# Ten more probability tiles split by GpSimd, weight subtractions cut in halves, and the first pair's bit rows copied by ScalarE, in a fused attention and MoE kernel

## The chip, the cores and the metric

The kernel runs on one core of one Trainium2 chip, as one program. The metric is the device time of one execution in microseconds. The kernel before took 852.72 us (median of 3 executions, 852.25 to 853.36).

## What is computed

Three layers follow each other. The first is attention in which a query sees only the keys that fall into the same hash bucket; the second and third are two feed-forward layers. Inputs are float32; 2 batches, 8 heads, 768 positions, head size 64.

```python
q_bits = (np.einsum('bhsd,dk->bhsk', q, proj) > 0)      # 6 bits, k_bits alike
mask = q_bucket[:, :, :, None] == k_bucket[:, :, None, :]
scores = np.where(mask, scale * np.matmul(q, k.transpose(0, 1, 3, 2)), -1e9)
attn = np.exp(scores - scores.max(-1, keepdims=True))
attn = attn / (attn.sum(-1, keepdims=True) + 1e-09)
x = np.matmul(attn, v)
...
xn = x / np.sqrt(np.mean(x * x, -1, keepdims=True) + 1e-06) * rms_g
x = (silu(xn @ w_gate) * (xn @ w_val)) @ w_out          # 512 -> 1536 -> 512
...
out = elu(x @ w_in) @ w_out                             # 512 -> 2048 -> 512
```

## The kernel before

**Split numbers.** TensorE multiplies operands of type float32r. Where full accuracy is wanted, a float32 tile is split into a rounded upper part (made by a cast) and the rest (made by a subtraction), and products are summed over two or three passes. So nearly every tile that goes to TensorE needs a cast, mostly on ScalarE, and a subtraction, mostly on VectorE.

**Attention.** Two heads make a pair, eight pairs in all (`j`). `prep` makes the operands of a pair: `twice` copies a head's rows next to themselves into `rd` (L334); `prep_T` transposes halves of `rd` on TensorE (L350), ScalarE makes the upper part `tq` or `tk` from the PSUM bank (L356), VectorE the rest (L361), and GpSimd copies the lower half of `tq` into two further places, `again` (L368) and `across` (L371). `prep_bits` and `prep_count` compute the hash bits and turn them into extra rows of the operands (L398 to L430), so that scores in other buckets come out far too small. The bits of a pair need all `across` copies of that pair.

A pair has six units `u`, each of two score tiles of 128 x 768. For each tile TensorE computes scores (L477), VectorE the row maximum `nm` (L484), ScalarE the exponential `p` (L494). Then `turn` transposes the unit's probabilities in three pieces `n` (L522), and each piece is split into `pt`: ScalarE casts it from PSUM (L530) and VectorE subtracts (L534). The pieces `n == 0` of the units listed in `BYPOOL` go another way: ScalarE copies the bank to SBUF as `pf` (L539), GpSimd casts (L543) and subtracts (L546). `weigh` multiplies with the values (L569), three pieces into one PSUM bank, in the order 1, 2, 0 for the units in `BYPOOL`; ScalarE and VectorE join the halves into `ot` (L583, L587). `post` scales by the reciprocal sums `r` (L605, L610) and `norm` makes the normed activations `xn` of a batch: for the first batch on GpSimd (L699 to L746), while the pairs 4 and 5 run, for the second on VectorE and ScalarE after pair 7.

**Feed-forward.** Eleven groups of hidden columns. `weights` loads a float64-wide tile, brings it to float32 with one instruction of ScalarE (L811) and four of VectorE (L814, L820, L827, L834, all within SBUF), then splits it: ScalarE casts (L855), GpSimd subtracts (L859). The weights of the first group are converted while the last three pairs run. `hidden` (L908 to L958), `reduce1` (L993) and `reduce2` (L1048) follow.

**Order.** Every piece of work is given to `Plan.add` with its engine, an estimated duration, what it reads and writes, and a priority. `Plan.order` is a list scheduler that runs in Python when the program is built: it keeps a clock for each engine, starts whatever can start first, breaks ties by priority, and the instructions are issued in that order, which is fixed for each engine's in-order queue. The table `OFF` shifts priorities by kind of work and pair. PSUM has four single banks (`bank`) and two double ones; `pt` has four buffers, the half-size pool `h3` nine.

Of the kernel before, what the change touches and what calls it, by code (L numbers as in the profile page):

```python
# [24 lines left out]
POOL_COPY = 0.82  # L25
FIRST = ('Pool', 'DVE', 'Pool', 'ACT')
# [3 lines left out]
BYPOOL = ([0, 1, 2, 3, 4], [0, 2, 3, 4], [0, 1, 2, 3, 4, 5], [2, 4], [2, 4], [2, 4], [2, 4], [0])  # L30
HOT = ('DVE', 'ACT', 'ACT', 'DVE')
BW = (384, 512)
OFF = {'S': [-0.746, -0.843, -1.864, 66.85, -0.744, -0.758, -0.224, -0.41], 'max': [86.06, 128.957, 190.513, 53.124, 102.143, -5.035, -10.834, 24.749], 'exp': [119.567, 67.059, 76.291, 2.774, 75.069, 56.662, -35.846, 43.868], 'T': [0.573, 0.48, 0.307, 0.831, 0.703, 1.127, 1.259, 1.321], 'hi': [36.303, -33.663, 1.961, -57.136, 22.322, 57.959, -91.469, -121.974], 'lo': [-34.121, 9.653, 32.465, -109.77, -12.636, -87.223, -67.192, -11.818], 'V': [2.027, 1.953, 1.894, 2.015, 1.865, 2.222, 2.417, -11.303], 'my': [76.979, -114.216, -55.16, -8.134, -134.423, -45.978, -63.486, -29.752], 'ld': [16.116, 103.645, 134.666, -130.684, 51.199, 277.906, -45.786, 44.455], 'pv': [19.903, -68.605, 49.828, -156.296, 63.827, 116.499, -168.838, 19.653], 'prep': [-0.809, -2.78, -3.346, -0.341, -0.21, -0.194, 0.226, -82.459], 'post': [4.851, 4.774, 2.643, 1.592, 3.332, 9.244, 3.712, 28.29], 'plo': [-227.264, -10.728, 0.013, -54.307, -64.379, -36.39, 74.399, -48.961], 'wc': 0.693, 'ld1': 50.459, 'norm0': -125.474, 'rush': 27.318, 'pstep': 0.316, 'qstep': 0.146, 'norm': -8.853, 'w0': 189.461, 'w0s': 3.7229545865993564e+29}


class Plan:

# [142 lines left out]
def kernel(  # L180
# [1086 lines left out]
```

## Time and profile before

| | us |
|---|---|
| median of 3 executions | 852.72 |
| the profiled execution's own time | 852.93 |
| its span, first to last instruction | 851.1 |
| TensorE busy | 832.4 (98%) |
| VectorE busy | 638.5 (75%) |
| ScalarE busy | 444.9 (52%) |
| GpSimd busy | 273.3 (32%) |

The 1.8 us between span and time lie before the first and after the last instruction. The shares are means over two very different stages: attention, to about 290 us, in which three or four engines are busy nearly all the time, and the feed-forward layers, in which TensorE runs almost alone. They have to be read stage by stage.

### The profile page before, as it was taken

Reading aid. Unit: us, or ns where it says so; the run is one execution under the profiler, and the core shown is the slowest. Engines: PE = TensorE matmul, PEld = TensorE weight load, DVE = VectorE, ACT = ScalarE, POOL = GpSimd, SP = SyncE. Lnnn points to the kernel's source line nnn. Section 1 sums busy time; section 2 is a strip of 40 time slices with the busy share of each in tenths; the row PEclk is TensorE's granted clock in tenths of the full one; section 3 lists DMA queues with packets and bytes.
Section 4 is the critical chain, followed back from the end, with each engine's and each line's share of the span. In section 5 each row is a group of like instructions: output and inputs, shape, how many; then the busy total and the mean of one; then the engine's idle time right before and its main releaser. Section 6 shows DMA issues by size and latency. Waiting matters only on the chain.

```text
span 851.1 us, 12464 instructions
## 1 busy us (share of the span) xinstructions
PE 832.4 (98%) x4722; PEld 736.7 (87%) x4722; DVE 638.5 (75%) x1015; ACT 444.9 (52%) x838; POOL 273.3 (32%) x289
## 2 busy tenths in 40 slices
PE   8999999998999999999999999999999999999998
PEld 7999999887998899999889898887888888888786
DVE  6999899999999987534364565579857778676754
ACT  6988988898987664432222322235444333332321
POOL 7857476789824312111011111110201101111100
PEclk9999999999999999999999999999999999999999
DMA  5102012330002200310111312213121302001003
GB/s 168 41 17 75 2 38 75 121 122 1 20 1 75 75 13 26 112 50 1 56 48 46 100 50 100 75 33 128 62 75 37 112 25 75 25 30 46 1 12 137
DMA packets 25708, 49.05 MB, mean 58 GB/s; under 512 B 2480, under 2 KB 8880, under 8 KB 25648
## 3 DMA queue, kind: packets, MB, share of 16 engines
q1 hardware_dynamic: 25648, 48.25, 17.3%
q8 instruction: 37, 0.61, 0.3%
q14 instruction: 23, 0.19, 0.1%
HBM read 45.09 MB, written 3.15 MB: 57 GB/s over the span
## 4 chain that ended last, share of the span: by engine, by line
PE 81%; DVE 13%; ACT 4%; issue 1%; POOL 1%; ACTq 0%; DVEq 0%; POOLq 0%
PE ps_h L908 37%; PE ps_o L1048 14%; PE ps_y L993 11%; PE ps_p L522 5%; PE ps_v L569 5%; PE ps_s L477 4%; DVE nm L484 3%; DVE pt L534 3%; PE ps_t L350 2%; PE ps_b L398 2%; ACT p L494 1%; ACT pt L530 1%; DVE wf L827 1%; DVE wf L834 1%; PE ps_w L1153 1%
## 5 line engine op out<-in xcount | busy, mean ns | idle before, releaser
L859 POOL TENSOR_TENSOR wlo<-wf,whi 128x768 fp32r<-128x768 f32 (+1 forms) x54 | 86.8, 1607 | 442.9 <-ACT whi L855 430.6
L908 PE MATMUL ps_h<-xn,whi 128*128 128x512 f32 (+2 forms) x768 | 190.2, 337 | 0.8 <-DVE hf L939 0.7
L908 PEld LDWEIGHTS ps_h<-xn,whi 128*128 128x128 f32 x768 | 133.5, 189 | 13.2 <-DVE hf L939 1.1
L908 PE MATMUL ps_h<-xn,wlo 128*128 128x256 f32 (+2 forms) x384 | 128.9, 336 | 0.0
L1048 PE MATMUL ps_o<-whi,h 128*128 128x512 f32 (+1 forms) x388 | 118.7, 387 | 0.8 <-DVE oa L1060 0.8
L908 PE MATMUL ps_h<-y,whi 128*128 128x512 f32 x384 | 118.2, 389 | 0.0
L933 ACT ACTIVATE sg<-ps_h 128x512 f32<-128x512 f32 (+1 forms) x87 | 50.7, 583 | 116.6 <-PE ps_h L908 114.5
L855 ACT CAST whi<-wf 128x768 fp32r<-128x768 f32 (+1 forms) x54 | 39.6, 733 | 118.2 <-DVE wf L834 118.2
L569 PE MATMUL ps_v<-pt,vv 128*128 128x256 f32 x576 | 96.8, 295 | 4.1 <-DVE pt L534 3.2
L954 ACT CAST h<-hf 128x512 fp32r<-128x512 f32 (+1 forms) x87 | 51.6, 605 | 88.1 <-DVE hf L939 49.1
L993 PE MATMUL ps_y<-h,whi 128*128 128x512 f32 (+1 forms) x312 | 91.4, 374 | 1.5 <-DVE ya L1005 1.5
L484 DVE TENSOR_REDUCE nm<-ps_s 128x1 f32<-128x768 f32 x96 | 90.6, 945 | 1.6 <-PE ps_s L477 0.9
L958 DVE TENSOR_TENSOR h<-hf,h 128x512 fp32r<-128x512 f32 (+1 forms) x87 | 71.0, 831 | 26.9 <-ACT h L954 26.2
L494 ACT ACTIVATE p<-ps_s,nm 128x768 f32<-128x768 f32 x96 | 87.2, 909 | 5.5 <-DVE nm L484 4.4
L522 PE MATMUL ps_p<-ident,p 128*128 128x128 f32 x576 | 86.0, 275 | 3.3 <-DVE pt L534 1.5
L477 PE MATMUL ps_s<-tk,tq 128*128 128x384 f32 x384 | 87.9, 350 | 0.6 <-ACT tk L428 0.4
L1048 PEld LDWEIGHTS ps_o<-whi,h 128*128 128x128 f32 x388 | 72.2, 188 | 16.4 <-DVE oa L1060 1.9
L569 PEld LDWEIGHTS ps_v<-pt,vv 128*128 128x128 f32 x576 | 79.3, 189 | 7.2 <-DVE pt L534 5.1
L908 PEld LDWEIGHTS ps_h<-y,whi 128*128 128x128 f32 x384 | 72.1, 188 | 15.0
L939 DVE TENSOR_TENSOR hf<-ps_h,sg 128x512 f32<-128x512 f32 (+1 forms) x39 | 25.2, 647 | 78.5 <-PE ps_h L908 78.5
L534 DVE TENSOR_TENSOR pt<-ps_p,pt 128x512 fp32r<-128x512 f32 x120 | 79.9, 680 | 2.7 <-ACT pt L530 1.8
L908 PEld LDWEIGHTS ps_h<-xn,wlo 128*128 128x128 f32 x384 | 72.6, 189 | 5.5
(111 smaller groups left out, 1501.0 us busy)
## 6 DMA issues: line engine op xcount, KB each, us to landing
wraw<-in_moe_w_out_dram SPq DMA_DIRECT2D x12, 768.0 KB, 4.9
wraw<-in_moe_w_in_dram SPq DMA_DIRECT2D x8, 768.0 KB, 4.6
wraw<-in_moe_w_out_dram SPq DMA_DIRECT2D x10, 512.0 KB, 4.1
raw<-in_q_dram SPq DMA_DIRECT2D x16, 192.0 KB, 3.4
raw<-in_k_dram SPq DMA_DIRECT2D x16, 192.0 KB, 3.7
vn<-in_v_dram SPq DMA_DIRECT2D x8, 384.0 KB, 3.3
wraw<-in_moe_w_gate_dram SPq DMA_DIRECT2D x4, 768.0 KB, 4.4
wraw<-in_moe_w_val_dram SPq DMA_DIRECT2D x4, 768.0 KB, 4.6
```

The costliest lines, as they stand in the source:

```text
L477: nc.tensor.matmul(st[B_][:, hf, 0:HS], lhsT=tq[:, x, c * 128:(c + 1) * 128], rhs=tk[:, x, hf * HS:(hf + 1) * HS], start=(x == 0), stop=(x ...
L484: nc.vector.tensor_reduce(out=st["nm", u, cc], in_=st[B_][:, :, 0:HS], axis=AX.XY, op=ALU.max, negate=True,)
L494: nc.scalar.activation(out=halves(st["p", u][:, cc]), in_=st.pop(B_)[:, :, 0:HS], func=AF.Exp, bias=st["nm", u, cc], scale=1.0, accum_out= ...
L522: nc.tensor.transpose(out=st[B_][:, o:o + 128], in_=p[:, cc, (2 * n + kt) * 128:(2 * n + kt + 1) * 128], identity=ident,)
L534: nc.vector.tensor_tensor(out=pt[:, 1], in0=st.pop(B_), in1=f(pt[:, 0]), op=ALU.subtract)
L569: nc.tensor.matmul(st[B_][:, 0:256], lhsT=st["vv", j][:, a, 2 * n + kt, :], rhs=pt[:, x, kt * 256:(kt + 1) * 256], start=(n == seq[0] and ...
L859: nc.gpsimd.tensor_tensor(out=l, in0=s["w"], in1=f(h), op=ALU.subtract)
L908: nc.tensor.matmul(ps[:, o:o + ln], lhsT=w[wp][:, kk, ft * 128:(ft + 1) * 128], rhs=t[xp][:, s:s + ln], start=(kk == 0 and n == 0), stop=( ...
L954: nc.scalar.copy(out=st["h", g, blk, ft][:, 0, 0:bw], in_=s["hf"])
L958: nc.vector.tensor_tensor(out=h[:, 1, 0:bw], in0=s["hf"], in1=f(h[:, 0, 0:bw]), op=ALU.subtract)
L993: nc.tensor.matmul(s["ps"][:, 0:bw], lhsT=wo[wp][:, ft, m * 128:(m + 1) * 128], rhs=h[:, xp, 0:bw], start=(ft == 0 and i == 0), stop=(ft = ...
L1048: nc.tensor.matmul(s["ps"], lhsT=h[:, xp, t * 128:(t + 1) * 128], rhs=wo[wp][:, ft, ds], start=(ft == 0 and i == 0), stop=(ft == n - 1 and ...
```

## The change

Five things are changed. (1) `BYPOOL` lists ten more units: pairs 3 to 7 have 3, 3, 4, 6 and 3 instead of 2, 2, 2, 2 and 1. (2) The subtraction of the weights on GpSimd (L859) is issued as two instructions over half a tile each. (3) In pair 0 the `across` copies are made by ScalarE from the PSUM bank, not by GpSimd from SBUF, and VectorE's subtraction for `tk` then covers 64 partitions. (4) In pair 0 the four `twice` copies are made by VectorE, ScalarE, ScalarE, VectorE instead of GpSimd, VectorE, GpSimd, ScalarE. (5) VectorE tasks whose operands all lie in SBUF are entered in the plan with 0.2 us more (`port=True`); with other entries of `OFF` and some other estimates this gives another order on every engine. `AGAIN` and `NORM` keep what was done before.

```diff
-POOL_COPY = 0.82
-FIRST = ('Pool', 'DVE', 'Pool', 'ACT')
+POOL_COPY = 0.79
+FIRST = ('DVE', 'ACT', 'ACT', 'DVE')
...
-BYPOOL = ([0, 1, 2, 3, 4], [0, 2, 3, 4], [0, 1, 2, 3, 4, 5], [2, 4], [2, 4], [2, 4], [2, 4], [0])
+BYPOOL = ([0, 1, 2, 3, 4], [0, 2, 3, 4], [0, 1, 2, 3, 4, 5], [1, 2, 4], [1, 3, 5], [0, 2, 4, 5], [0, 1, 2, 3, 4, 5], [0, 1, 4])
+AGAIN = ('Pool', 'Pool', 'Pool', 'Pool', 'Pool', 'Pool', 'Pool', 'Pool')
+ACROSS = ('ACT', 'Pool', 'Pool', 'Pool', 'Pool', 'Pool', 'Pool', 'Pool')
+NORM = ('Pool', 'DVE')
...
-OFF = {'S': [-0.746, -0.843, -1.864, 66.85, ...
+OFF = {'S': [-1.867, -1.487, -1.644, 46.711, ...
...
+    SHARED = 0.2
...
+        if port and eng == "DVE":
+            self.tasks[i] = (eng, us + self.SHARED, *self.tasks[i][2:])
...
-            m = (up, slice(0, 128))[i]
+            m = up if i == 0 else dn if ACROSS[j] == "ACT" else slice(0, 128)
...
-        def across():
-            nc.gpsimd.tensor_copy(out=operand(j, a, 1)[up, 1, cs], in_=f(operand(j, a, 0)[dn, 0, cs]))
+        def under():
+            to = operand(j, a, 1)[up, 1, cs]
+            if ACROSS[j] == "ACT":
+                nc.scalar.activation(out=to, in_=st[B_][up, 0:HS], func=AF.Copy, scale=sc)
+            else:
+                nc.gpsimd.tensor_copy(out=to, in_=f(operand(j, a, 0)[dn, 0, cs]))
...
-        def lo():
+        def lo(x):
             h, l = (wpart(t, g, m, part) for t in st["w", g][nm])
-            nc.gpsimd.tensor_tensor(out=l, in0=s["w"], in1=f(h), op=ALU.subtract)
+            if shape[1] % 2 == 0:
+                z = (slice(None), slice(x * shape[1] // 2, (x + 1) * shape[1] // 2))
+            else:
+                z = (slice(None), slice(None), slice(x * shape[2] // 2, (x + 1) * shape[2] // 2))
+            nc.gpsimd.tensor_tensor(out=l[z], in0=s["w"][z], in1=f(h[z]), op=ALU.subtract)
```

Two places show how the order moves. The first is GpSimd's queue behind the norm of batch 0, in pairs 4 and 5: `xn` ends the norm, `pt` is a probability tile (cast, then subtraction), `tq` and `tk` are the copies that the bits of pair 6 wait for. Before:

```order
L746 TENSOR_TENSOR xn<-xT,xn 128x384
L543 CAST pt<-pf 128x512
L746 TENSOR_TENSOR xn<-xT,xn 128x384
L546 TENSOR_TENSOR pt<-pf,pt 128x512
L543 CAST pt<-pf 128x512
L368 CAST tq<-tq 64x384
L546 TENSOR_TENSOR pt<-pf,pt 128x512
L368 CAST tq<-tq 64x384
L371 CAST tk<-tq 64x384 x2
L368 CAST tq<-tq 64x384 x2
L371 CAST tk<-tq 64x384 x2
```

With the change:

```order
L767 TENSOR_TENSOR xn<-xT,xn 128x384 x2
L564 CAST pt<-pf 128x512 x2
L567 TENSOR_TENSOR pt<-pf,pt 128x512 x2
L564 CAST pt<-pf 128x512
L377 CAST tq<-tq 64x384
L567 TENSOR_TENSOR pt<-pf,pt 128x512
L564 CAST pt<-pf 128x512
L639 COPY rw<-r 128x768
L567 TENSOR_TENSOR pt<-pf,pt 128x512
L377 CAST tq<-tq 64x384
L384 CAST tk<-tq 64x384 x2
L377 CAST tq<-tq 64x384 x2
```

Four tiles instead of two, and the copy `rw`, now stand between the norm and the `tk` copies (two more of which follow the last row shown).

The second is VectorE's queue from behind the last row maximum of attention to the last probability tiles: `wf` are the conversions of the weights, `hf` belongs to the first hidden unit. Before:

```order
L827 SCALAR_TENSOR_TENSOR wf<-wraw,wf 128x768
L820 TENSOR_SCALAR wf<-wf 128x768
L605 TENSOR_SCALAR r<-sums 128x12
L834 SCALAR_TENSOR_TENSOR wf<-wraw,wf 128x768
L610 RECIPROCAL r<-r 128x12
L827 SCALAR_TENSOR_TENSOR wf<-wraw,wf 128x768
L587 TENSOR_TENSOR ot<-ps_v,ot 64x256
L939 TENSOR_TENSOR hf<-ps_h,sg 128x384
L814 TENSOR_SCALAR wf<-wf 128x768
L834 SCALAR_TENSOR_TENSOR wf<-wraw,wf 128x768
L534 TENSOR_TENSOR pt<-ps_p,pt 128x512 x3
```

With the change:

```order
L835 TENSOR_SCALAR wf<-wf 128x768
L555 TENSOR_TENSOR pt<-ps_p,pt 128x512
L608 TENSOR_TENSOR ot<-ps_v,ot 64x256
L555 TENSOR_TENSOR pt<-ps_p,pt 128x512
L841 TENSOR_SCALAR wf<-wf 128x768
L626 TENSOR_SCALAR r<-sums 128x12
L848 SCALAR_TENSOR_TENSOR wf<-wraw,wf 128x768
L631 RECIPROCAL r<-r 128x12
L855 SCALAR_TENSOR_TENSOR wf<-wraw,wf 128x768
L608 TENSOR_TENSOR ot<-ps_v,ot 64x256
L967 TENSOR_TENSOR hf<-ps_h,sg 128x384
L555 TENSOR_TENSOR pt<-ps_p,pt 128x512 x3
```

Four conversions instead of six stand there, and none between `hf` and the last three tiles.

## Rows read from the trace of the kernel before

**Rows 1.** Busy time by 25 us: PE, PEld, DVE, ACT, POOL (instructions), clock, DMA.

```profile
175.00:200.00 25.00, 21.60 (x153) 18.84 (x151) 24.54 (x40) 24.72 (x53) 22.74 (x23) 1.00 0.22 71
200.00:225.00 25.00, 23.38 (x164) 21.22 (x164) 23.87 (x40) 21.61 (x45) 23.56 (x29) 1.00 0.05 16
225.00:250.00 25.00, 24.55 (x181) 23.32 (x181) 24.76 (x41) 21.79 (x47) 10.57 (x15) 1.00 0.00 1
250.00:275.00 25.00, 23.04 (x170) 21.95 (x169) 24.76 (x37) 19.40 (x40) 11.54 (x7) 1.00 0.20 65
275.00:300.00 25.00, 23.00 (x146) 21.71 (x146) 24.75 (x37) 16.20 (x27) 8.87 (x5) 1.00 0.19 64
```

**Rows 2.** Groups of TensorE, 225 to 300 us: busy, mean ns | idle before, releaser.

```profile
L569 PE MATMUL ps_v<-pt,vv 128*128 128x256 f32 x144 | 24.1, 296 | 3.2 <-DVE pt L534 3.2
L522 PE MATMUL ps_p<-ident,p 128*128 128x128 f32 x136 | 19.6, 274 | 0.3 <-DVE xT L636 0.3
L908 PE MATMUL ps_h<-xn,whi 128*128 128x384 f32 x64 | 16.7, 341 | 0.8 <-DVE hf L939 0.7
L477 PE MATMUL ps_s<-tk,tq 128*128 128x384 f32 x73 | 16.5, 345 | 0.1
L908 PE MATMUL ps_h<-xn,wlo 128*128 128x384 f32 x32 | 10.7, 335 | 0.0
```

**Rows 3.** Chain that ended last, 244 to 305 us: start, duration, what.

```profile
271.81 2.11 PE ps_h L908 x12
273.93 1.43 PE ps_v L569 x12
275.35 0.70 PE ps_s L477 x4
276.06 1.32 PE ps_p L522 x12
...
285.01 2.52 DVE wf L834
```

**Rows 4.** Groups of VectorE, 214.9 to 284 us, first row maximum of pair 6 to `hf`.

```profile
L534 DVE TENSOR_TENSOR pt<-ps_p,pt 128x512 fp32r<-128x512 f32 x35 | 23.1, 679 | 0.2
...
L827 DVE SCALAR_TENSOR_TENSOR wf<-wraw,wf 128x768 int32<-128x768 int32 x4 | 3.7, 929 | 0.0
```

**Rows 5.** Groups of GpSimd, 0 to 300 us.

```profile
L546 POOL TENSOR_TENSOR pt<-pf,pt 128x512 fp32r<-128x512 f32 x24 | 32.3, 1348 | 1.3
...
L543 POOL CAST pt<-pf 128x512 fp32r<-128x512 f32 x24 | 15.4, 642 | 41.2 <-ACT pf L539 38.1 <-ACT pt L530 2.1 <-POOL tk L371 0.6
```

**Rows 6.** Timeline of GpSimd, 163 to 208 and 284 to 289 us: start, duration, instruction.

```profile
163.78 1.01 POOL L699 TENSOR_TENSOR z<-z,y 128x384 f32<-128x384 f32 x1 [1.17 <-ACT y L694]
...
197.23 1.02 POOL L746 TENSOR_TENSOR xn<-xT,xn 128x384 fp32r<-128x384 f32 x1
198.20 2.17 POOL L546 TENSOR_TENSOR pt<-pf,pt 128x512 fp32r<-128x512 f32 x1
...
205.81 1.59 POOL L371 CAST tk<-tq 64x384 fp32r<-64x384 f32 x2
...
284.79 1.92 POOL L859 TENSOR_TENSOR wlo<-wf,whi 128x768 fp32r<-128x768 f32 x1 [0.62 <-ACT whi L855]
```

**Rows 7.** One line of VectorE, L605, whole span: duration ns min/median/max.

```profile
L605 DVE TENSOR_SCALAR r<-sums x8: 161/242/1209, 47.1 to 281.5; 128x12 f32<-128x12 f32 x8
```

**Rows 8.** Timeline of ScalarE and TensorE in the first 13 us.

```profile
4.63 0.84 ACT L1115 ACTIVATE bitt<-ident 1x768 fp32r<-1x768 f32 x1
5.80 0.83 ACT L334 COPY rd<-raw 128x768 f32<-128x768 f32 x1 [0.32 <-DMA raw<-in_k_dram]
...
9.71 0.87 ACT L356 ACTIVATE tq<-ps_t 128x384 fp32r<-128x384 f32 x2
...
12.61 0.44 PE L398 MATMUL ps_b<-tk,pj 128*128 128x384 f32 x1 [0.56 <-POOL tk L371]
```

More of the change, by code (lines that the diff above doesn't have):

```diff
@@ L50, in __init__, with add @@
         self.last_w, self.readers, self.touch, self.duty = {}, {}, {}, {}
-    def add(self, eng, us, fn, r=(), w=(), prio=None, lat=0.0, tab=None, duty=1.0):
+    def add(self, eng, us, fn, r=(), w=(), prio=None, lat=0.0, tab=None, duty=1.0, port=False):
         i = len(self.tasks)
@@ L336, in twice @@
         us = {"Pool": POOL_COPY, "DVE": dve(S), "ACT": act(S) + 0.04}[eng]
-        plan.add(eng, us, go, [(("slot", "raw", j), i, a)], [("h3", "rd", j, a, i)], prio)
+        plan.add(eng, us, go, [(("slot", "raw", j), i, a)], [("h3", "rd", j, a, i)], prio, port=eng == "DVE")
     def prep_T(j, a, i, hf, prio):
@@ L612, in post @@
         sums = [(("sum", j), a, c) for a in range(2) for c in range(NC)]
-        plan.add("DVE", 0.1, plus, sums, [R_], prio)
-        plan.add("DVE", 0.17, inv, [], [R_], prio)
+        plan.add("DVE", 0.08, plus, sums, [R_], prio, port=True)
+        plan.add("DVE", 0.14, inv, [], [R_], prio, port=True)
         def widen():
@@ L751, in norm @@
                 if late:
-                    plan.add("DVE", dve(HS) + 0.06, scale, [(Y_, hf), "gsc"], [F_], p + step)
+                    plan.add("DVE", dve(HS) + 0.06, scale, [(Y_, hf), "gsc"], [F_], p + step, port=True)
                 else:
@@ L914, in wkeys @@
     def wkeys(g, m):
-        return [(("slot", x, g, m), p) for x in ("whi", "wlo") for p in range(2)]
+        return [(("slot", "whi", g, m), p) for p in range(2)] + [
+            (("slot", "wlo", g, m), p, x) for p in range(2) for x in range(2)
+        ]
     def hidden(g, blk, ft, prio):
@@ L1025, in reduce1 @@
             plan.add("ACT", act(bw) + 0.043, hi, ak, [*yk[0], (Y_[1], "got", blk)], prio)
-            plan.add("DVE", dve(bw), lo, ak + yk[0], yk[1], prio)
+            plan.add("DVE", dve(bw), lo, ak + yk[0], yk[1], prio, port=True)
     def reduce2(g, blk, t, prio):
@@ L1140 @@
     plan.add("Pool", 1.22, setup, [], ["ident", "pj0"], -30)
-    plan.add("DVE", 0.7, setup_w, [], [("h3", "wtmp")], -30)
-    plan.add("DVE", 2.2, setup_count, [("h3", "wtmp")], [("h3", "ctmp")], -30)
+    plan.add("DVE", 0.5, setup_w, [], [("h3", "wtmp")], -30, port=True)
+    plan.add("DVE", 1.0, setup_count, [("h3", "wtmp")], [("h3", "ctmp")], -30, port=True)
     plan.add("Pool", 0.25, setup2, [], ["wsel0"], -29.5)
@@ L1156 @@
         plan.add("PE", 0.218, lambda n=n: warm(n), ["ident"], [("bank", "warm")], 1e6)
-    plan.add("DVE", 2.2, setup_pj, [("pjf", a) for a in range(2)] + ["pj0"], ["pj"], -29)
+    plan.add("DVE", 0.6, setup_pj, [("pjf", a) for a in range(2)] + ["pj0"], ["pj"], -29, port=True)
     wk = []
```

52 lines of the change are left out of this document (32 added, 20 removed).

## Prediction

> **What bounds the kernel now.** I read the busy time by stretches first. From about 300 us on TensorE works without a break and the change hardly touches what it does there, so the end of the kernel is where attention ends plus a constant. Before that, look at the last five stretches of attention [rows 1]. VectorE is busy 23.9 to 24.8 of each 25 us. ScalarE has 24.7 in the first of them and then falls to 16.2; GpSimd has 22.7 and 23.6 in the first two and then 8.9 to 11.5. TensorE has idle time in each: 3.4, 1.6, 0.5, 2.0 and 2.0 us, 9.5 in all. So there are two different stages. From 175 to 225 us (the second half of pair 4, all of pair 5) three engines are full at once; from 225 to 300 us VectorE alone is.
>
> The idle time understates what TensorE loses, because a matmul counts as busy while it waits in the pipe. For 225 to 300 us I add up what its work takes without a wait, from pieces of the chain in which it ran back to back: 0.176 us for one `ps_h`, 0.119 for `ps_v`, 0.175 for `ps_s`, 0.110 for `ps_p` [rows 3]. By the counts of that stretch [rows 2] this is 96 x 0.176 + 144 x 0.119 + 73 x 0.175 + 136 x 0.110 = 61.8 us, and 44 small matmuls of other kinds at 0.11 to 0.175 add about 6: 68 of 75 us. TensorE thus loses about 7 us there, and what ended its waits was VectorE: 3.2 us for `pt`, 0.7 for `hf` [rows 2]. This is the ceiling of what relief of VectorE can bring in that stretch.
>
> **The change part by part.** *Pairs 6 and 7.* From the first row maximum of pair 6 to `hf`, VectorE subtracts 34 tiles of `pt` in the order before and 28 in the new one; the other rows of its queue differ by one conversion less and one join more, which about cancel. A tile costs 23.1/35 = 0.66 us there [rows 4], so 6 x 0.66 = **-4.0 us** on the engine that has 0.2 us of idle time in a stretch of 25. ScalarE still copies each tile out of PSUM, as it did. GpSimd gets 1.35 + 0.64 = 1.99 us for each tile [rows 5], 12 us in 70, and has 13 us free in each 25 [rows 1]. The bounds are 0 (if those tiles then arrive late) and -7 (if the whole loss goes).
>
> *Pairs 4 and 5.* VectorE has three subtractions less, -2.0 us, but the new order puts two conversions of weights more into these pairs, some 1.9 at 0.93 each [rows 4]: nothing is won. GpSimd is the question. Its queue runs from the start of the norm at 163.8 us almost without a gap until the last `tk` copy of pair 6 ends at 205.8 + 1.6 = 207.4 [rows 6], and TensorE's bits of pair 6, with all of pair 6 behind them, wait for that copy. The order of the change has two more tiles between the norm's end and these copies, 4.0 us, and one more copy. TensorE, in order, stands if they are late. They need not be: the bits come one unit of pair 5 earlier in TensorE's queue than before, so other work is left to do, and what the wait costs is partly what ScalarE at 24.7 of 25 would cost anyway. I bound this from -2.0 (VectorE's three tiles pay in full) to +4.0 (both tiles shift pair 6) and take the middle, **+1.0**.
>
> *The hand-over.* Near the end of attention one conversion of VectorE took 2.52 us in the chain [rows 3], where a like one of the same size takes 0.93 [rows 4]; GpSimd's weight subtraction of 1.92 us began 0.2 us before it [rows 6]. Three probability tiles and TensorE behind them stood for it. In the new order no conversion lies between `hf` and those three tiles, and a subtraction over half the weights holds VectorE half as long. That is 2.52 - 0.93 = 1.6 us on the path; the bounds are 0 (another conversion is held in its place, of four that are left) and -3.9 (all waits of TensorE for VectorE in that stretch [rows 2]). I take **-1.5**, near the row.
>
> This is where a rule bears. The row first: L605 works on 12 numbers a partition, all in SBUF, and took from 161 to 1209 ns, with a median of 242 [rows 7]; an instruction of that size is not slow, it was held. The Trainium skill, page "SBUF — State Buffer", section "Who interferes with whom", says that a VectorE instruction with two SBUF inputs, or in a two-port mode, and a GpSimd instruction that reads SBUF exclude each other for a whole instruction, whichever started first. The trace agrees, with the 2.52 us conversion beside the 1.92 us subtraction. By that rule the halves help and the ten tiles, 20 us more of reading by GpSimd, harm; the subtractions of `pt` that VectorE keeps read PSUM and go free. The sum above has no term for the harm; it is the third rival.
>
> *The start.* GpSimd loses two copies and four `across`; ScalarE takes one copy and the four rows, VectorE one copy. ScalarE is busy with constants until 5.47 us, so its two copies end near 7.1 instead of 5.80 + 0.83 = 6.6, and then it makes 12 halves instead of 8 at 0.87/2 = 0.44 each: 7.1 + 5.2 = 12.3 us. Before, TensorE's bits waited for the `across` copy until 12.61 [rows 8]. VectorE's last subtraction has still to follow, 0.5 or so. So **0**, within -1 and +1. Pairs 0 to 3 get one tile more and another order; nothing in it is worth more than the 1 us either way already allowed, and I add **0**.
>
> *The feed-forward layers* get twice as many GpSimd subtractions of half the length, beside a full TensorE: **0**, within -1 and +1 (one hold by a subtraction of 1.9 us avoided, or half a tile late for a group).
>
> The sum is -4.0 + 1.0 - 1.5 = -4.5 us against the profiled execution of 852.93 us, so 848.4; that execution was 0.2 above the median of the three, so I predict **848.2 us**.
>
> **The rivals.** *GpSimd becomes the bound in pairs 4 and 5.* For it: 22.7 and 23.6 of 25 us, and one queue from 163.8 to 207.4 us. Two tiles late is 4.0, the `rw` copy ahead of them and a held subtraction (2.17 against 1.35 us [rows 5, 6]) make it 5.0 in place of my +1.0. The sum is then -0.5: 852.2 us, no change. Against it: attention's other engines are just as full there, so the delay is shared. Chance 0.17.
>
> *All of TensorE's loss from 225 us on goes.* Then the two later terms give -7 instead of -5.5, and pairs 4 and 5 give their full -2.0: -9.0, 843.7 us. For it: VectorE is what TensorE waits for. Against: the queues are fixed and some waits move. Chance 0.15.
>
> *GpSimd's tiles hold VectorE.* The mechanism of the rows on L605 and the 2.52 us: in pairs 6 and 7 each of six tiles holds one conversion or one `r` of VectorE, each of which stands ahead of row maxima, for up to a subtraction of 1.35 us: 8.1 us. The sum becomes +3.6, **856.3 us, slower**. It decides from the point at which 4.5/1.35, between three and four, of the tiles meet such an instruction. For it: VectorE has no slack for it, and a dozen conversions are in these pairs. Against: GpSimd's busy share rises only from some 45% to about 60% of these pairs, and four of the long conversions there averaged 0.93 us as it was [rows 4]. Chance 0.13.
>
> That the change does not do what it says can be left out: the orders show the tiles moved.
>
> **How the numbers follow.** The forecast as worked out keeps 0.55, with a range of its own from 846 to 851 us. A measurement of this kernel tells a difference from about 0.2%, 1.7 us. Faster by more than that, below 851.0, are nearly all of the forecast's cases and the second rival: 0.70. Within 0.2% falls the first rival: 0.17. Slower, above 854.4, is the third: 0.13. The range from 843.5 to 853.2 us leaves out the third rival and the best of the second.
>
> **What would show it.** Right: VectorE has 110 `pt` subtractions instead of 120 and the first `hf` comes some 4 us earlier, at about 280 us; no conversion of VectorE takes over 2 us near the hand-over; TensorE's idle time from 225 to 300 us falls from 4.4 to about 2 us. For the first rival: the bits of pair 6 wait on `tk` of GpSimd, 3 us or more after 207. For the third: the conversions in pairs 6 and 7 average well over 1.3 us, and `r` over 1. Wrong at the root would be a first hidden unit that comes no earlier, or a time won or lost after 300 us by more than 1 us.

## The result, and the profile after

The changed kernel takes **858.53 us** (median of 4 runs, 857.42 to 858.56) against 852.8 us of the kernel before in the same session: ratio 1.0064, 95% interval 1.0047 to 1.0082. It is slower, by 0.64%; the forecast was 848.2 us, faster. The profiled execution took 858.56 us, its span is 856.8 us. One of the four executions took 857.42 us at a mean granted clock of 1.000, the other three 858.53 to 858.56 us at 0.997 to 0.998, so a difference of 1 us between single executions says little.

Where the time went is read from landmarks that both traces have: the start of the first row maximum (`nm`) of each pair, and the end of the last one. Each row is one profiled execution.

| us | pair 0 | pair 4 | pair 6 | pair 7 | last `nm` ends | span |
|---|---|---|---|---|---|---|
| before | 17.2 | 138.2 | 214.9 | 245.9 | 278.4 | 851.1 |
| after | 21.5 | 143.1 | 225.2 | 260.8 | 286.3 | 856.8 |

The differences from one landmark to the next: the start costs 4.3 us, pairs 0 to 3 0.6, pairs 4 and 5 **5.4** (82.1 against 76.7). Pairs 6 and 7 gain 2.4 and the feed-forward layers 2.2 (570.5 against 572.7). The sum is +5.7.

The busy time by stretches answers to [rows 1] (PE, PEld, DVE, ACT, POOL with instructions, granted clock, DMA):

```profile
0.00:25.00 25.00, 19.26 (x111) 16.79 (x112) 16.49 (x43) 17.15 (x33) 13.91 (x29) 0.93 0.47 143
...
175.00:200.00 25.00, 20.21 (x138) 17.07 (x138) 23.54 (x33) 22.17 (x48) 23.47 (x24) 1.00 0.37 123
200.00:225.00 25.00, 19.15 (x125) 15.90 (x124) 22.91 (x36) 18.19 (x36) 21.92 (x27) 1.00 0.00 1
225.00:250.00 25.00, 24.29 (x177) 22.51 (x176) 24.40 (x39) 21.50 (x46) 23.95 (x29) 1.00 0.06 18
250.00:275.00 25.00, 23.01 (x173) 21.46 (x173) 24.34 (x36) 20.61 (x42) 19.60 (x18) 1.00 0.11 31
275.00:300.00 25.00, 25.00 (x185) 24.83 (x184) 22.89 (x39) 19.43 (x39) 11.41 (x9) 1.00 0.30 98
```

TensorE's idle time from 175 to 225 us went from 5.0 us [rows 1] to 10.6. GpSimd, which had 13 us or more free in each of the stretches from 225 us on, is now busy 23.95 us in the first of them. From 275 to 300 us TensorE has no gap any more.

VectorE's groups in pairs 4 and 5, 143.1 to 225.2 us after (busy, mean ns | idle before):

```profile
L555 DVE TENSOR_TENSOR pt<-ps_p,pt 128x512 fp32r<-128x512 f32 x30 | 19.8, 679 | 0.4
...
L848 DVE SCALAR_TENSOR_TENSOR wf<-wraw,wf 128x768 int32<-128x768 int32 x3 | 3.8, 1264 | 0.0
L855 DVE SCALAR_TENSOR_TENSOR wf<-wraw,wf 128x768 int32<-128x768 int32 x2 | 3.5, 1734 | 0.0
L835 DVE TENSOR_SCALAR wf<-wf 128x768 f32<-128x768 f32 x4 | 3.4, 872 | 0.0
L841 DVE TENSOR_SCALAR wf<-wf 128x768 int32<-128x768 int32 x3 | 3.1, 1040 | 0.0
```

and the same groups before, 138.2 to 214.9 us:

```profile
L534 DVE TENSOR_TENSOR pt<-ps_p,pt 128x512 fp32r<-128x512 f32 x33 | 21.9, 677 | 0.6 <-ACT pt L530 0.5
...
L827 DVE SCALAR_TENSOR_TENSOR wf<-wraw,wf 128x768 int32<-128x768 int32 x2 | 2.3, 1158 | 0.0
...
L820 DVE TENSOR_SCALAR wf<-wf 128x768 int32<-128x768 int32 x3 | 2.2, 723 | 0.0
L814 DVE TENSOR_SCALAR wf<-wf 128x768 f32<-128x768 f32 x3 | 1.9, 662 | 0.2 <-ACT wf L811 0.2
L834 DVE SCALAR_TENSOR_TENSOR wf<-wraw,wf 128x768 int32<-128x768 int32 x2 | 1.9, 942 | 0.0
```

Three subtractions less save 2.1 us. The conversions of weights (the rows of `wf`) went from 10 steps in 8.3 us to 12 steps in 13.8: two steps more, and each some 40% longer (1.15 us on average against 0.83). What lengthens them stands in the timeline of VectorE and GpSimd after, near the end of pair 5:

```profile
208.12 1.27 POOL L567 TENSOR_TENSOR pt<-pf,pt 128x512 fp32r<-128x512 f32 x1
208.16 2.04 DVE L855 SCALAR_TENSOR_TENSOR wf<-wraw,wf 128x768 int32<-128x768 int32 x1
209.34 1.34 POOL L564 CAST pt<-pf 128x512 fp32r<-128x512 f32 x1
...
211.18 2.24 DVE L835 TENSOR_SCALAR wf<-wf 128x768 f32<-128x768 f32 x2
211.41 1.59 POOL L567 TENSOR_TENSOR pt<-pf,pt 128x512 fp32r<-128x512 f32 x1
```

The conversion at 208.16 us begins 0.04 us behind a tile's subtraction on GpSimd and ends 0.81 us behind that one's end; in pairs 6 and 7 the same step takes 0.95 us on average. So I read that it stood until GpSimd was done. GpSimd's next instruction, a cast that averages 0.64 us [rows 5], then takes 1.34. That is the alternation which the Trainium skill, page "SBUF — State Buffer", section "Who interferes with whom", describes: whichever of the two comes first keeps the shared ports for its whole instruction. The trace agrees, in both directions. VectorE's subtractions of `pt`, which read one operand from PSUM and one from SBUF, took 677 ns before and 679 after: they go free, as that section of the Trainium skill says of a VectorE instruction with at most one SBUF input.

The chain that ended last runs through these conversions (start, duration, what):

```profile
203.96 1.22 DVE wf L841
206.64 1.03 DVE wf L848
208.16 2.04 DVE wf L855
211.25 2.17 DVE wf L835 x2
216.72 0.95 PE ps_v L590 x8
218.23 2.20 PE ps_b L419 x12
```

The last row is TensorE's bits of pair 6. GpSimd's `tk` copies for them had been done more than 1 us earlier:

```profile
215.85 0.96 POOL L384 CAST tk<-tq 64x384 fp32r<-64x384 f32 x2
```

Before, the bits did not wait for such a copy either. They came behind ScalarE's copy `pf`, which empties a PSUM bank, and the `tk` copies that ended at 207.4 us [rows 6] landed while they ran (chain before):

```profile
206.50 0.49 ACT pf L539
207.04 2.35 PE ps_b L398 x12
```

So the path that the prediction took for pairs 4 and 5, from GpSimd's queue through `tk` to the bits, carried the time in neither kernel.

### The profile page after: what moved, and what is told of

It is laid out like the page before. It is cut to its first block, busy times and chain, and to the rows that moved or that the text cites. A ratio compares the mean times of both kernels' runs of the same rounds, so it can differ in the third digit from the quotient of the medians.

```text
span 856.8 us, 12525 instructions
## 1 busy us (share of the span) xinstructions
PE 832.8 (97%) x4722; PEld 737.5 (86%) x4722; DVE 627.7 (73%) x1006; ACT 445.5 (52%) x841; POOL 308.6 (36%) x357
## 4 chain that ended last, share of the span: by engine, by line
PE 87%; ACT 5%; POOL 3%; DVE 3%; issue 2%; POOLq 0%; ACTq 0%
PE ps_h L934 39%; PE ps_o L1076 15%; PE ps_y L1021 12%; PE ps_v L590 6%; PE ps_p L543 6%; PE ps_s L498 5%; PE ps_t L356 2%; PE ps_b L419 2%; ACT p L515 1%; ACT pt L551 1%; DVE pt L555 1%; PE ps_c L440 1%; POOL xT L752 0%; POOL xT L753 0%; PE ps_x L648 0%
## 5 line engine op out<-in xcount | busy, mean ns | idle before, releaser
L884 POOL TENSOR_TENSOR wlo<-wf,whi 128x384 fp32r<-128x384 f32 (+1 forms) x108 | 104.7, 990 | 426.5 <-ACT whi L876 363.7
L590 PE MATMUL ps_v<-pt,vv 128*128 128x256 f32 x576 | 94.5, 294 | 1.8 <-DVE pt L555 1.8
L543 PE MATMUL ps_p<-ident,p 128*128 128x128 f32 x576 | 84.2, 275 | 7.8 <-DVE ot L608 3.2
L543 PEld LDWEIGHTS ps_p<-ident,p 128*128 128x128 f32 x576 | 66.3, 140 | 14.9 <-DVE ot L608 4.0
L986 DVE TENSOR_TENSOR h<-hf,h 128x512 fp32r<-128x512 f32 (+1 forms) x87 | 64.8, 759 | 19.0 <-ACT h L982 18.2
L555 DVE TENSOR_TENSOR pt<-ps_p,pt 128x512 fp32r<-128x512 f32 x110 | 73.8, 682 | 5.5 <-ACT pt L551 4.1
```

Of the source, the lines that this page charges most:

```text
L543: nc.tensor.transpose(out=st[B_][:, o:o + 128], in_=p[:, cc, (2 * n + kt) * 128:(2 * n + kt + 1) * 128], identity=ident,)
L555: nc.vector.tensor_tensor(out=pt[:, 1], in0=st.pop(B_), in1=f(pt[:, 0]), op=ALU.subtract)
L590: nc.tensor.matmul(st[B_][:, 0:256], lhsT=st["vv", j][:, a, 2 * n + kt, :], rhs=pt[:, x, kt * 256:(kt + 1) * 256], start=(n == seq[0] and ...
L884: nc.gpsimd.tensor_tensor(out=l[z], in0=s["w"][z], in1=f(h[z]), op=ALU.subtract)
L986: nc.vector.tensor_tensor(out=h[:, 1, 0:bw], in0=s["hf"], in1=f(h[:, 0, 0:bw]), op=ALU.subtract)
```

## The experiments

All tests take the kernel after and change its tables, and most fix the order of its tasks in a written list, so that nothing else is decided anew:

```diff
+ORDER = [
...
+]
     def run(self):
-        for i in self.order():
+        for i in ORDER:
             self.tasks[i][2]()
```

The list is put together from the orders of before and of after, cut at the first score of pair 0, 4 or 6. Each median below stands beside the median of before from the same session (852.3 to 852.8 us).

### The parts of the change, one at a time

**Only the halves.** Tables and order of before:

```diff
-FIRST = ('DVE', 'ACT', 'ACT', 'DVE')
+FIRST = ('Pool', 'DVE', 'Pool', 'ACT')
-BYPOOL = ([0, 1, 2, 3, 4], [0, 2, 3, 4], [0, 1, 2, 3, 4, 5], [1, 2, 4], [1, 3, 5], [0, 2, 4, 5], [0, 1, 2, 3, 4, 5], [0, 1, 4])
+BYPOOL = ([0, 1, 2, 3, 4], [0, 2, 3, 4], [0, 1, 2, 3, 4, 5], [2, 4], [2, 4], [2, 4], [2, 4], [0])
-ACROSS = ('ACT', 'Pool', 'Pool', 'Pool', 'Pool', 'Pool', 'Pool', 'Pool')
+ACROSS = ('Pool', 'Pool', 'Pool', 'Pool', 'Pool', 'Pool', 'Pool', 'Pool')
```

> As before in everything, also in the order, except that each weight subtraction of GpSimd is cut into two of half the columns, one right behind the other. Theory (a shorter hold of VectorE's conversions at the hand-over and in the feed-forward layers): 852.8 - 2.5 = 850.3 us, and the conversion that took 2.52 us at the hand-over takes 1.7 or less. Rival 1 (what TensorE lost in the feed-forward layers came from the order, not from the length of a subtraction): 852.8. Rival 2 (two starts in place of one on a full queue): 853.5.

Measured: **849.13 us**, ratio 0.9962 (0.9950 to 0.9975). The theory holds: 3.1 us gained. In the trace the last `nm` ends 0.7 us earlier and the rest takes 570.3 us against 572.7. The held conversion at the hand-over (2.52 us in the chain of [rows 3]) was before

```profile
284.92 2.60 DVE L834 SCALAR_TENSOR_TENSOR wf<-wraw,wf 128x768 int32<-128x768 int32 x1
```

and here it is

```profile
284.03 2.79 POOL L1034 TENSOR_TENSOR wlo<-wf,whi 128x384 fp32r<-128x384 f32 x2 [0.60 <-ACT whi L1026]
...
284.19 1.77 DVE L1005 SCALAR_TENSOR_TENSOR wf<-wraw,wf 128x768 int32<-128x768 int32 x1
```

It now stands for the first half only, and takes 1.77 us; the two halves took 2.79 us together where the one subtraction took 1.92 [rows 6], so I read that GpSimd's second half waited in its turn.

**Only the start undone** (`FIRST` and `ACROSS` as above, order of before up to the first score):

> The kernel after, but everything up to the first score of pair 0 is as before (who copies the rows, who writes the bit rows of pair 0, and the order of that stretch); from there on the order of after. Theory (the parts of the change add up; the start costs what the first row maximum shows, 21.5 against 17.2 us): 858.5 - 4.3 = 854.2 us, the last hidden unit 4.3 us earlier than after. Rival 1 (later waits on DMA loads or on the engines' own queues take the delay in anyway): 858.5 and the pairs close up again by pair 2. Rival 2 (the order behind was fitted to that start, and waits elsewhere): between 855 and 858.

Measured: 855.50 us, ratio 1.0041 (1.0027 to 1.0054): 3.2 us above before, where after stood 5.7. The start costs some 2.5 us, less than its landmark (4.3) said; this is rival 2's range (855 to 858), not the theory's 854.2. The profiled execution took 857.32 us, 1.8 above the median, so its landmarks are not those of the median: its first row maximum came at 19.7 us, and TensorE was granted 0.85 and 0.50 of its clock in the two stretches from 15 to 20 us there.

**Only pairs 4 and 5 undone**, with their order (in `BYPOOL`):

```diff
...
-[1, 3, 5], [0, 2, 4, 5],
+[2, 4], [2, 4, 5],
...
```

> The kernel after, but pairs 4 and 5 (from the first score of pair 4 to that of pair 6) in the order of before and with GpSimd splitting tiles 2 and 4 of pair 4 and 2, 4 and one of the last two of pair 5; start, pairs 0 to 3, 6, 7 and feed-forward as after. Theory (the three more tiles and the two more conversions of weights in these pairs cost 5.4 us): 858.5 - 5.4 = 853.1 us; from the first row maximum of pair 4 to that of pair 6 77 us instead of 82. Rival 1 (the loss only moved out of pairs 6 and 7, whose conversions come earlier in after): 853 to 854 is not reached, since pairs 6 and 7 here have neither these conversions nor a lighter GpSimd: 858. Rival 2 (holds of VectorE by GpSimd's tiles everywhere in the later pairs): about half of it, 856.

Measured: 855.31 us, ratio 1.0033 (1.0020 to 1.0046). Pairs 4 and 5 take 77.5 us, as expected, but pairs 6 and 7 take 64.1 instead of 61.1. Of the 5.4 us some 2.7 are won in the end, about half: rival 1 in part, and nearest to rival 2's number. This middle has 12 steps of conversion too, and they take 9.7 us instead of 13.8: two steps and one tile more than before cost 0.8 us (77.5 against 76.7), so the number of steps alone is not the loss.

**Only the tail of after** (`FIRST` and `ACROSS` as above; in `BYPOOL`):

```diff
...
-[1, 2, 4], [1, 3, 5], [0, 2, 4, 5],
+[2, 4], [2, 4], [2, 4, 5],
...
```

> As before up to the first score of pair 6 (one tile of pair 5 more by GpSimd), from there on as after: eight tiles of pairs 6 and 7 by GpSimd instead of three, weights subtracted in halves, the order of after. Theory (the later pairs gain 2.4 us and the feed-forward layers 2.3 us): 852.8 - 4.7 = 848.1 us. Rival 1 (GpSimd's tiles hold VectorE in pairs 6 and 7, and after gained there only because pair 6 came late and had its data ready): 852.8 or slower, up to 856. Rival 2 (only the feed-forward part gains): 850.5.

Measured: 850.88 us, ratio 0.9982 (0.9973 to 0.9991). This is rival 2 (only the feed-forward part gains, 850.5). The halves alone are 1.75 us better, so the tiles and the order of pairs 6 and 7 gain nothing. Pair 6 takes 37.8 us here, against 31.0 before; pair 7 25.5 against 32.5. GpSimd is busy 35.9 of the 37.8 us of pair 6, and TensorE stands for it at 215 to 220 us (the stretch, then TensorE's wait from 200 to 240 us, then GpSimd):

```profile
215.00:220.00 5.00, 1.90 (x11) 1.46 (x11) 4.82 (x7) 1.54 (x4) 4.94 (x5) 1.00 0.29 79
```

```profile
PE ps_p L693 <- ACT pf L710: 2.4, 1, 2.4
```

```profile
212.79 3.12 POOL L825 TENSOR_TENSOR sq<-xT 128x768 f32<-128x768 f32 x1
...
216.84 2.97 POOL L1034 TENSOR_TENSOR wlo<-wf,whi 128x384 fp32r<-128x384 f32 x2
```

ScalarE's copy `pf` for a GpSimd tile waits for a buffer that GpSimd has yet to empty: it starts at 219.84 us, as that subtraction `wlo` ends.

The parts do not simply add up. Undone one at a time, the start gives 2.5 us back and pairs 4 and 5 2.7; with both undone, and pairs 0 to 3 (0.6 us) with them, it is 7.1.

### Tiles or order?

In each half of the later pairs the tiles were changed without the order, and the order without the tiles; a moved tile's instructions stand where those that they replace stood.

Pairs 6 and 7, on the halves alone, nine tiles instead of three in the order of before (the expectations count eight):

```diff
...
-[2, 4], [0])
+[0, 1, 2, 3, 4, 5], [0, 1, 4])
```

> As the run with the halves alone (order of before, subtractions of weights in halves), but GpSimd splits eight tiles of pairs 6 and 7 instead of three; each extra tile's two GpSimd instructions stand where VectorE's subtraction stood. Theory (the tiles themselves relieve VectorE; what cost time in pair 6 was that the order of after also puts the row squares and twice as many weight subtractions into GpSimd's queue there): 849.1 - 5 x 0.66 = 845.8 us. Rival 1 (GpSimd's tiles hold VectorE's conversions, or come late for TensorE, whatever else stands in its queue): 849 to 851. Rival 2 (TensorE in these pairs is bound by something else): 849.1 with VectorE's busy time 3 us lower.

and three tiles in the order of after, on the tail of after (the one tile more of pair 5 is undone with them):

```diff
...
-[2, 4, 5], [0, 1, 2, 3, 4, 5], [0, 1, 4])
+[2, 4], [2, 4], [0])
```

> As the run with the tail of after (before up to the first score of pair 6, order of after from there), but GpSimd splits only three tiles of pairs 6 and 7, as before; VectorE gets the other five back. Theory (GpSimd, busy 36.5 of pair 6's 37.7 us in that run, is its bound there; without four of its tiles, some 8 us, pair 6 gets shorter): 850.9 - 3 = 848 us, pair 6 in 34 us or less. Rival 1 (the order of after costs the time in pair 6, by five conversions instead of one on VectorE, and the tiles relieve it): 852 to 854. Rival 2 (the loss is at the seam of the two orders, at 215 to 220 us, before the tiles count): 850.9.

Measured: 852.79 us (ratio 0.9999, 0.9990 to 1.0008) and 853.39 us (1.0011, 1.0003 to 1.0020). From the first row maximum of pair 6 to the end of the last: 62.7 us with order and tiles of before (the halves alone), 65.3 with the tiles of after, 66.2 with the order of after, 63.2 with both. Each alone costs 2.6 or 3.5 us, both together 0.5. Neither theory holds: the tiles don't win by themselves (852.79 is above the first run's rivals too), and the order without its tiles is slower, which is rival 1 of the second run. The order does better with the tiles it was made with.

Pairs 4 and 5, in the same way, in the kernel after:

```diff
...
-[1, 3, 5], [0, 2, 4, 5],
+[1, 3], [2, 4, 5],
...
```

> The kernel after, its order kept, but in pairs 4 and 5 GpSimd splits five tiles instead of seven (the last tiles of pair 4 and the first of pair 5 go back to VectorE). Theory (the loss in pairs 4 and 5 is GpSimd's queue, which the two tiles lengthen): 858.5 - 3 = 855.5 us, the last bit-row copy of pair 6 some 3 us earlier. Rival 1 (it is the order, which puts conversions of weights beside GpSimd's norm and tiles; held time of the conversions stays at 5 us): 858.5 or slower by the 1.3 us that VectorE gets.

and all tiles of after in the order of before (of the list, these two pairs):

> The kernel after, with all its tiles, but pairs 4 and 5 in the order of before (each tile's instructions moved in place). With the run above and the one with the whole middle of before (855.3 us) it separates tiles from order. Theory (tiles lengthen GpSimd's queue): no gain against after, 858 to 859. Rival 1 (the order of the conversions is what costs): 855.3 us, as with the whole middle of before; held time of the conversions of these pairs falls from 5.3 us to 1.5.

Measured: 858.81 us (1.0072, 1.0059 to 1.0084) and 859.46 us (1.0074, 1.0062 to 1.0087): nothing came back. The pairs take 82.1 and 82.4 us, where both changes undone gave 77.5. The first theory falls; the second holds, and with it falls its rival that the order is what costs. The 12 conversions take 11.6 us in either, 2.2 less than in after, and VectorE is busy 76.0 and 74.9 us instead of 76.8, yet the pairs are no shorter. So the loss could not be divided into a tiles part and an order part, and shorter conversions were not enough to win it back.

### What bounds pairs 4 and 5

Three steps of conversion (`c5` of the second weight piece, `c2` of the third and fourth) were put behind the first score of pair 6; of the order:

```diff
-weights.c5, weights.hi, weights.c2, weights.c2
 score.pe of unit 36
 post.inv of pair 5
+weights.c5, weights.hi, weights.c2, weights.c2
```

> The kernel after, but the last three steps of weight conversion that VectorE does in pair 5 (one of them took 2.04 us, two together 2.24 us in after) and the weight copy behind them stand behind the first score of pair 6. Theory (the held conversions lengthen pairs 4 and 5, where three engines are full): pair 4 to 6 some 2 to 3 us shorter than 82.1 us, and 856 us if pair 6, where VectorE is less full, takes them at their unheld 0.9 us each. Rival 1 (GpSimd's queue, with the norm and seven tiles, is the bound of pairs 4 and 5): 82 us again, 858.5. Rival 2 (they are held as long in pair 6): pairs 4 and 5 shorter, pair 6 longer, 858.5.

Measured: 859.00 us (1.0079, 1.0066 to 1.0091). The moved steps took 1.02 us instead of 2.04 and 1.11 instead of 2.24, and nothing was won, a miss. TensorE's bits of pair 6 did come at 216.0 instead of 218.2 us; but the moved steps stand ahead of the first row maximum of pair 6 now, which came at 225.6 us (225.2 in after). So work was taken away instead.

Without VectorE's conversion of three weight pieces (the guard stands in `c2` to `c5`):

```diff
+LEAVE = ((0, 0, 0), (0, 0, 1), (0, 1, 0))
...
             def c2():
+                if (g, m, part) in LEAVE:
+                    return
```

> The kernel after, but VectorE's four steps of the conversion of the first three weight pieces (11 of the 12 steps in pairs 4 and 5) are left out, so that these weights are the absolute upper words times 0.02 and the output is another one. VectorE has some 12.5 us less to do in pairs 4 and 5. Theory (GpSimd's queue, with norm, tiles and copies, bounds pairs 4 and 5): they take 80 us or more (82.1 in after). Rival 1 (VectorE bounds them): 75 us or less. Rival 2 (three full engines in turn): 77 to 79.

Without eight multiplications of GpSimd in these pairs (the expectation says twelve; GpSimd's instructions there go from 80 to 72):

```diff
                     nc.gpsimd.tensor_tensor(out=x, in0=x, in1=st["y", b][:, xs[2]], op=ALU.mult)
-                    nc.gpsimd.tensor_tensor(
-                        out=x, in0=x, in1=gsc[:, kk:kk + 1].to_broadcast([128, HS]), op=ALU.mult
-                    )
```

> The kernel after, but GpSimd's multiplication by the gain in the normalization of the first batch is left out (12 instructions of 0.83 to 1.43 us), so that the output is another one. GpSimd has 8 to 10 us less to do in pairs 4 and 5. Theory (GpSimd's queue bounds them): 74 to 76 us instead of 82.1, and 851 us. Rival 1 (VectorE does): 81 to 82 us. Rival 2 (three full engines in turn): 78 to 80.

And without both:

> Both left out: VectorE's conversion of the first three weight pieces and GpSimd's multiplication by the gain in the first normalization; the output is another one. Theory (GpSimd's queue bounds pairs 4 and 5): as with the multiplication alone, 74 to 76 us. Rival 1 (VectorE does): as without the conversions alone. Rival 2 (one takes the other's place): 70 to 72 us, more than the two single gains together.

Measured: 851.35 us (0.9989, 0.9979 to 0.9998), 856.83 us (1.0049, 1.0034 to 1.0064) and 851.85 us (0.9993, 0.9984 to 1.0003). Pairs 4 and 5 as one stretch, with columns as above. Before:

```profile
138.20:214.90 76.70, 71.59 (x502) 63.80 (x501) 73.07 (x120) 69.12 (x145) 65.78 (x75) 1.00 0.23 76
```

After:

```profile
143.10:225.20 82.10, 71.42 (x492) 62.52 (x491) 76.76 (x119) 68.60 (x143) 69.92 (x80) 1.00 0.24 73
```

Without the conversions:

```profile
143.20:219.60 76.40, 70.40 (x486) 61.90 (x485) 65.43 (x108) 68.09 (x142) 66.00 (x80) 1.00 0.25 78
```

Without the multiplications:

```profile
142.20:223.20 81.00, 71.03 (x492) 62.35 (x491) 77.15 (x119) 68.73 (x143) 63.14 (x72) 1.00 0.23 74
```

With 11.3 us less on VectorE the pairs are 5.7 us shorter; with 6.8 us less on GpSimd 1.1; with both 76.4 us again. My theory (GpSimd's queue) fell in all three, and rival 1 is the nearest: **VectorE's work is what lengthens pairs 4 and 5**. Two things limit this. 76.4 us is above the 75 that rival 1 had set: only half of the 11.3 us left out comes back, so something else bounds the pairs by then. And GpSimd is busy 3.9 us less without the conversions, though its instructions are the same 80: as I read it, the time it was held went with them. VectorE was busy 73.1 of 76.7 us there before and is busy 76.8 of 82.1 after, although three tiles were taken from it; 1.7 us of the 5.4 are idle time of VectorE, which it has more than before.

### The start

Only the row copies as before, then only the bit rows as before, with the order of after:

```diff
-FIRST = ('DVE', 'ACT', 'ACT', 'DVE')
+FIRST = ('Pool', 'DVE', 'Pool', 'ACT')
```

> The kernel after, its order kept, but the four row copies of pair 0 are made as before (GpSimd, VectorE, GpSimd, ScalarE); the bit rows of pair 0 stay with ScalarE. Theory (of the 3 us that the start costs, the wait of VectorE's subtraction for ScalarE's bit-row copy is the larger part): 857.5 to 858, first row maximum 0.5 to 1 us earlier than after's 21.5 us. Rival (two row copies on ScalarE, which is busy with constants until 5.5 us, are the cost): 855.5 us, as with the whole start of before.

```diff
-ACROSS = ('ACT', 'Pool', 'Pool', 'Pool', 'Pool', 'Pool', 'Pool', 'Pool')
+ACROSS = ('Pool', 'Pool', 'Pool', 'Pool', 'Pool', 'Pool', 'Pool', 'Pool')
```

> The kernel after, its order kept, but GpSimd writes the bit rows of pair 0 again; the row copies stay as after. Theory (VectorE's subtraction waits for ScalarE's bit-row copy, 0.4 to 0.5 us each, and TensorE's transposes wait for VectorE): 856 us, first row maximum 2 us earlier than after's 21.5 us. Rival (the row copies are the cost): 858 to 858.5.

Measured: 858.73 us (1.0072, 1.0060 to 1.0085) and 860.59 us (1.0095, 1.0081 to 1.0109). With the row copies the first row maximum comes at 20.3 us instead of 21.5, but the time is no shorter, so the rival falls; the bit rows make it worse, so my theory falls with it. Then nine more warm-up products where TensorE had stood:

```diff
-WARM = 16
+WARM = 25
```

> The kernel after, but with nine more warm-up products on TensorE, three ahead of the seventh transpose (where TensorE had no work for 0.69 us) and six ahead of the tenth (1.31 us); the result of a warm-up is not used. Theory (the clock granted at 7.5 to 12.5 us, 0.65 and 0.67, follows from these two gaps): granted clock 1.00 there, 857.4 us, as in the one run of after whose mean clock was 1.000. Rival 1 (the clock falls whatever TensorE does there): 858.5. Rival 2 (the warm-ups delay the transposes): 859.

Measured: 858.69 us (1.0070, 1.0057 to 1.0083). In after TensorE waited from 5.7 to 6.4 and from 7.2 to 8.5 us, and these stretches show the clock (last column but two):

```profile
5.00:7.50 2.50, 1.47 (x12) 1.04 (x10) 0.56 (x1) 2.48 (x5) 0.00 (x0) 1.00 0.08 20
7.50:10.00 2.50, 1.53 (x7) 1.54 (x8) 2.04 (x9) 1.94 (x5) 1.01 (x2) 0.65 0.39 106
10.00:12.50 2.50, 2.50 (x18) 2.50 (x17) 1.11 (x3) 0.75 (x2) 0.20 (x1) 0.67 0.99 237
```

With the warm-ups:

```profile
7.50:10.00 2.50, 2.41 (x20) 2.06 (x19) 2.04 (x9) 1.94 (x5) 1.01 (x2) 1.00 0.36 100
10.00:12.50 2.50, 2.37 (x19) 2.22 (x20) 1.80 (x5) 1.78 (x5) 0.99 (x2) 1.00 1.06 263
...
17.50:20.00 2.50, 1.41 (x7) 1.41 (x7) 2.02 (x4) 1.74 (x4) 2.12 (x4) 0.74 0.18 63
20.00:22.50 2.50, 2.50 (x15) 2.40 (x14) 2.09 (x4) 0.95 (x3) 0.50 (x1) 0.58 0.00 0
```

The drop at 7.5 us is gone, as the theory says, and the first score comes 0.8 us earlier; but TensorE then stands for 0.9 and 1.1 us between 15.4 and 18.6 us, and the clock falls behind that. The time didn't change. Nor do the two waits decide the clock by themselves: in the run with five tiles in pairs 4 and 5, whose start is that of after, TensorE waited as long (0.8 and 1.3 us), and the clock stayed:

```profile
5.00:7.50 2.50, 1.36 (x11) 0.94 (x9) 0.56 (x1) 2.48 (x5) 0.00 (x0) 1.00 0.07 17
7.50:10.00 2.50, 1.44 (x11) 1.25 (x11) 2.04 (x9) 1.94 (x5) 1.01 (x2) 1.00 0.41 115
```

The first row maximum came at 20.5 us there, 1.0 earlier than in after.

Last, the first transposes of pair 1, which wait for GpSimd's row copies, were put behind the first scores on TensorE, without and with the warm-ups; of the order:

```diff
-three prep_T.pe of pair 1, with their copies
 score.pe 0 to 2 of pair 0
+three prep_T.pe of pair 1, with their copies
```

> The kernel after, but on TensorE the first three transposes of pair 1 (with the copies that follow them) stand behind the first three scores of pair 0 instead of ahead of the first, as in before. Theory (these transposes wait for GpSimd's row copies of pair 1, and all scores behind them; that is most of the start's cost): first score near 18 instead of 19.9 us, first row maximum 19.5 to 20 instead of 21.5 us, 856.5 us. Rival (the scores have to wait for their own bit rows and row copies anyway, or the order behind takes it back): 858 to 858.5.

> The scores ahead of pair 1's transposes as in the run of that name, and the nine more warm-up products. Theory (the two add up: the clock of 7.5 to 12.5 us stays at 1.00, worth 1 us, and the scores come without the transposes): first row maximum 18.5 to 19 us, 855.5 us, as with the whole start of before (855.5 us). Rival (the clock falls later instead, at 17 to 22 us): as the run without the warm-ups, or 857.

Measured: 861.98 us (1.0113, 1.0099 to 1.0127) and 861.58 us (1.0111, 1.0096 to 1.0127), a miss. The first row maximum did come, at 18.1 and 18.3 us instead of 21.5, but TensorE then stood for the same row copies, in the first of the two:

```profile
26.40 1.54 PE L506 MATMUL ps_t<-ident,rd 128*128 128x128 f32 x6 [3.72 <-POOL rd L490]
```

Whether that is only because the copies kept their place in GpSimd's queue wasn't tried. The start's cost is shown as a whole (2.5 us); which part of it carries it stays open.

### A version that beats both

The halves alone up to the ninth product block of the feed-forward layers, then the order of after; tables and diff as in the halves alone, only the end of the list is another:

> The run with the halves alone up to the ninth product block of the feed-forward layers, from there on in the order of after; tiles, rows and bit rows as before. Theory (that run still lost about 2.4 us of TensorE's time at 300 to 325, 575 to 600 and 800 to 825 us, which the order of after does not lose): 849.1 - 2.0 = 847.1 us. Rival (the losses come from the hand-over and return elsewhere): 849.1.

Measured: **848.26 us**, ratio to before 0.9951 (0.9937 to 0.9965). That is 4 us below before, which is clear of the noise. The 0.9 us by which it is below the halves alone is not (the intervals overlap), and its theory had 2.0.

## Why the prediction was wrong

*Pairs 4 and 5, +1.0:* mis-sized, the largest part of the error; they cost 5.4 us. The step that failed is "the new order puts two conversions of weights more into these pairs, some 1.9 at 0.93 each [rows 4]: nothing is won". By it VectorE's account is even: 2.0 us of tiles saved, 1.9 of conversions added. Measured, the tiles save 2.1 and the conversions add 5.5 (13.8 against 8.3), and VectorE is busy 3.7 us longer. In the run with pairs 4 and 5 undone the same number of steps took 9.7 us and the pairs 77.5, near my +1.0; only with the tiles and the order of after do they cost 5.4. I priced the steps as in a place where GpSimd is half idle, while here it has 22.7 and 23.6 of 25 us [rows 1]. The wait was wrong too: "TensorE's bits of pair 6, with all of pair 6 behind them, wait for that copy" is shown by no row, the chain before goes through ScalarE. So I looked for the bound in GpSimd's queue, and the runs with work left out show that VectorE's work sets it. My own row of a held conversion [rows 3] and the rule of the Trainium skill beside it said what could happen; I used both for the hand-over and left them out of this sum.

*The third rival* had a mechanism that is there: GpSimd's tiles hold VectorE. It named 856.3 us, nearest of all to 858.5, with a chance of 0.13, but that is luck: its place was wrong (pairs 6 and 7 instead of 4 and 5), and its sign, conversions of well over 1.3 us on average in pairs 6 and 7, did not come: there nine took 8.0 us (one `r` did take 1.8). That holds lengthen the conversions of pairs 4 and 5 is shown by the timeline and the lengths; how much of the 5.4 us they are is open, since three runs with conversions 2 us shorter won nothing.

*Pairs 6 and 7, -4.0:* wrong. I took GpSimd's 13 us of free time in 25 [rows 1] for granted, but the order of the change also brings more row squares and more weight subtractions into pair 6 (7.8 us instead of 3.7), where GpSimd is busy 33.8 of 35.6 us. The 2.4 us that these two pairs gained in after are no gain of the tiles: put behind the middle of before, tail and tiles are 1.75 us slower than the halves alone.

*The hand-over, -1.5, and the feed-forward layers, 0:* the direction of the first was right, and the sum of both too small. The halves alone bring 3.1 us. The one conversion gave 0.8 (2.60 to 1.77); 0.7 came ahead of the last row maximum's end, and the rest behind the hand-over, where I took GpSimd's subtractions to be hidden behind a full TensorE: its idle time behind 300 us fell from 5.8 to 4.5 us with the halves alone. Both points under "wrong at the root" came true: the first `hf` comes at 292.8 us instead of 284.0, and TensorE's idle time behind 300 us fell by 1.8 us, to 4.0, in the change.

*The start, 0:* wrong, +2.5 us as a whole. I followed ScalarE's halves to 12.3 us and the bits of TensorE no further. In the trace VectorE's first subtraction waits for ScalarE's bit-row copy, TensorE's transposes for VectorE, and the first score came at 19.9 us instead of 15.2; that these waits are the cost is not shown, as the runs on the start won nothing.

*The first rival* (GpSimd the bound of pairs 4 and 5, 852.2): half of its sign came: the `tk` copies of pair 6 end at 216.8 instead of 207.4 us, but the bits did not wait for them. And 6.8 us less work on GpSimd bring only 1.1 us back, so its own load is not the bound. *The second*: TensorE's idle time from 275 to 300 us did go (2.0 to 0), 1.1 of it with the halves alone; from 225 to 275 us it stayed (2.4 to 2.7).

## What to carry to other kernels

Price an instruction that moves by what it costs where it lands, beside what the other engine does there, and not by its mean elsewhere; on an engine that is nearly full, two steps and some holds eat what three removed tiles gave. Before pricing a queue, look in the chain whether anything waits for its end. Where two engines hold each other up, cutting the longer instruction in two cost little and was most of the gain here. An order that was fitted to a placement can't be judged by undoing one of them: none of four such runs was better than with both kept, and all were worse than with both undone.

## What was not expected of the hardware

The clock granted to TensorE fell to 0.65 and 0.67 over 5 us, a mix of its two levels (1.2 and 2.4 GHz), right behind two waits of 0.7 and 1.3 us in the first 8.5 us; before, with warm-up products in that place, it stayed at 1.00. Filling the waits moved the fall to 17.5 us, behind the next waits. But another execution of the same start, with waits as long, kept 1.00 throughout: a fall may follow such waits and need not.

Holds go both ways: GpSimd's row squares over 128x768 took 3.12 us in one place of the run with the tail of after and 1.46 in another (VectorE's conversions and a reciprocal, 0.55, 0.89 and 0.22 us, ran beside the first), and its cast of a tile 1.34 instead of 0.64.
